# Reordered passages around a block-form dense stage: where the filler work, the PSUM banks, the weight loads and one query tile stand

## The chip, the cores and the metric

The kernel runs on one core of one Trainium2 chip. The metric is the device time of one execution in microseconds (us); lower is better. The engines are called PE (matmul), PEld (its weight loads), DVE (vector), ACT (scalar), POOL (GpSimd) and SP (the queue that issues nearly all transfers).

## The reference

Two branches of one input x (2048 rows of 640) are mixed by a gate per row, `g = sigmoid(x . gate_w)`:

```python
qkv = x @ wqkv                                # 32 heads of 20
phi(t) = [softmax(t @ w_phi), softmax(-t @ w_phi)]     # per head, for q and k
kv = phi(k).T @ v;  z = sum(phi(k))           # per head
a = (phi(q) @ kv) / (phi(q) @ z + 1e-6) @ wo
b = silu(x @ w1) @ w2                         # w1: 640 x 1728
out = g * a + (1 - g) * b
```

All of it is float32. The kernel gets near that precision by splitting an operand into a rounded high half and a low half (`split`, L117 on ACT and L119 on DVE or POOL: a cast, then a subtraction), and by three matmuls per product, high by high, high by low, low by high (`PASSES`).

## The kernel before

The work runs in four stages.

**Keys (about 0 to 173 us).** x goes by 16 tiles of 128 rows. For each tile `t` PE makes keys and values in the three PSUM banks `kvp[0..2]` (L497), DVE and ACT make the softmax features (`k_spikes`, Exp, `k_sums`), `k_split` splits them into `ph`, and two tiles later PE adds them up: `kv_acc` (L467) in five banks `kvt`, and `kv_rest` (L478) in a part of `kvp[2]`, called `krm`, which `kv_rest_sum` (L491, DVE) adds to a sum in SBUF after each tile. The table `ahead` hangs other work behind a tile: loading and splitting the first dense weights (`w_load(0)`, `w_sums(0)`, `w_parts(0, ..)`) and x for the dense stage (`n_split(b, c)`: block b of 512 rows, chunk c of 128 columns of D).

**Dense stage (about 173 to 372 us).** u = silu(x @ w1), stored to the DRAM tensor `u_d`. The 13 whole column tiles of w1 and the rest of 64 columns go two ways. The last whole tile ("l") and the rest ("r") are plain products: `h_std` (L537), 15 and 10 matmuls for a block of 512 rows. The other twelve are taken in pairs, with pairs of blocks, in a 2 x 2 block form with seven products instead of eight (a Strassen form). `h_pair(n, ..)` is one such unit, n = 0 to 11: n // 6 is the pair of blocks, n % 6 the pair of column tiles. Its seven products come in the order 1, 2, 6, 7, 4, 5, 3 (6, 9, 6, 6, 9, 9, 9 matmuls of 128 x 512: 54 in all, L583). Product 1 is copied to the tile `q` (ACT, L606); the others are added up by DVE (L597), and each of four results goes through Silu on ACT and a store (`u_out`, L548, L549). The weights of a unit are four split tiles a, b, c, d, made from two loaded tiles `wr` (L254, L255) and five POOL sums `wt` (`w_sums`, L270). The x operands are `n1`, `n2` and the split differences `t[1..4]`, made by `less` (L756) and `xt_first` for the first two blocks, and by `t_loads` (L1010), `t_sums` (POOL, L1027), `t_parts` and `n_parts` for the other two.

`between` is a table of the work that is traced behind a product of a unit (0: ahead of product 1); `plan(n)` fills it for the loads and splits of the next unit's weights. Unit 0 runs with `kvp[0]` and `kvp[1]` alone, since the key sums still hold the other banks; from unit 1 on all eight PSUM banks are used (`bank`). Ahead of unit 0 stand the two `h_std` groups of block 0 and of block 1, and the last key sums (`key_sums`) stand behind its product 1. `kv_out` (L646, L647, L652) writes the key sums out to `kv_d`. `r_out` (L553 to L556) finishes a rest group with a copy, an add, a Silu and a store.

**Queries (about 372 to 593 us).** Tiles 8 to 11 come first: `q_proj` (L455, 30 matmuls), `q_feat` (max, min, differences, Exp at L887), `q_sum`, `q_norm` (POOL, L901), `q_norm_sum` (L904), `q_small`, `q_mul` (POOL, L937), which leaves `es[t]`. Between them stand the `h_std` groups of blocks 2 and 3. `t_mm` (L1106) transposes `es` on PE, `t_out` (L1122, ACT) copies the result to `fT`, `n_mm` (L1187) multiplies with the key sums, `n_hi` and `n_lo` split that, and `w_mm` (L1220, "pa") multiplies with wo. `QT` is the list of the remaining query tiles; `step(u)` runs one group of 256 rows.

**Output (about 593 us on).** u is loaded again, split and multiplied with w2 (L1429), and the branches are mixed.

What sets the order: inside a block `with inorder(..)` the named engines run their instructions in the order of the code; each is a queue, and an instruction that waits holds up all behind it. The transfers on SP are in no such list: the planner places them by priority and by when a tile's buffer comes free, and SP then issues them one after the other, waiting where it must. A tile from a pool with `bufs` copies waits for the last reader of the copy that it takes: the pools "raw" (4), "ur" (2), "w" (9) and "u" (3) matter here.

## Time and profile before

| | us |
|---|---|
| median of 3 runs (785.01 to 786.8) | 785.77 |
| the profiled execution | 786.72 |
| its span in the profile | 784.9 |
| PE busy, share of the span | 746.2, 95% |
| PEld busy | 645.1, 82% |
| DVE busy | 448.2, 57% |
| ACT busy | 299.6, 38% |
| POOL busy | 323.4, 41% |

The mean granted clock of PE is 0.975 of full speed. Busy shares are means over stages: what a wait costs has to be read in its stage, from PE's rows in order of time. A row of PE gives its start, its length, the line, what it writes and reads, how many matmuls are merged in it, and in brackets how long PE was idle before and what released it. A merged row lasts until the end of its last matmul, which overlaps the next row a little. A row of SP lasts as long as SP was busy with or waited between the merged issues.

### The profile page before, as it was taken

The page shows a single profiled execution, that of the slowest core. Times are in us where ns is not written, and L with a number is a line of the kernel's source. Part 1 is how long each engine was busy: PE and PEld are TensorE (multiplying, and loading weights), DVE is VectorE, ACT ScalarE, POOL GpSimd, SP SyncE. Part 2 cuts the span into 40 slices and gives each one's busy share as a digit, 9 for nine tenths or more (in the row PEclk, how much of TensorE's full clock was granted, in tenths as well). Part 3 has the DMA queues.
Part 4 walks back from the last instruction along what each step waited for, and adds up shares of the span by engine and source line. Part 5 has one row for each costly group of instructions (what it writes and reads, how often), then busy time and mean ns, then how long its engine had stood idle before and what let it go on. Part 6 is the DMA issues. An engine that isn't in the chain of part 4 may idle for free.

```text
span 784.9 us, 10979 instructions
## 1 busy us (share of the span) xinstructions
PE 746.2 (95%) x4115; PEld 645.1 (82%) x4115; DVE 448.2 (57%) x760; ACT 299.6 (38%) x549; POOL 323.4 (41%) x231
## 2 busy tenths in 40 slices
PE   9999999997699979999975999999999999999997
PEld 7888888886488758888964999999998788888886
DVE  5667666786555566666865666767642452242413
ACT  5344444455334444445662353343441332111110
POOL 2479888655437633123274564563500030020300
PEclk9999999998899989999987999999999999999999
DMA  9221111101434285554310111220147676172511
GB/s 317 90 68 55 34 35 34 48 0 58 127 116 154 97 273 164 154 162 145 117 41 21 34 58 45 72 81 16 45 123 213 183 203 206 50 242 75 172 30 67
DMA packets 49663, 82.88 MB, mean 106 GB/s; under 512 B 5416, under 2 KB 18872, under 8 KB 49610
## 3 DMA queue, kind: packets, MB, share of 16 engines
q1 hardware_dynamic: 49322, 81.67, 33.5%
q8 instruction: 32, 0.52, 0.3%
q10 hardware_dynamic: 288, 0.51, 0.2%
q14 instruction: 21, 0.17, 0.1%
HBM read 56.90 MB, written 25.27 MB: 105 GB/s over the span
## 4 chain that ended last, share of the span: by engine, by line
PE 48%; DVE 4%; DMA 3%; POOL 1%; ACT 1%; issue 1%; SPq 1%; DVEq 0%; POOLq 0%; ACTq 0%
PE acc L1429 21%; PE pa L1220 9%; PE pq L455 7%; PE p L583 5%; PE pn L1187 3%; PE pT L1106 2%; DMA ur<-u_d 2%; DVE eq L446 1%; POOL eq L937 1%; DVE sm L904 1%; DMA w2rr<-w 1%; DMA u_d<-u 1%; DMA wo<-wo 1%; PE pwq L229 0%; DVE sm L891 0%
## 5 line engine op out<-in xcount | busy, mean ns | idle before, releaser
L1429 PE MATMUL acc<-u,w 128*128 128x512 f32 x780 | 178.3, 389 | 0.4 <-DVE u L119 0.2
L1429 PEld LDWEIGHTS acc<-u,w 128*128 128x128 f32 x780 | 146.3, 188 | 31.5 <-ACT u L117 0.6
L497 PE MATMUL kvp<-wh,xa 128*128 128x500 f32 (+1 forms) x420 | 92.9, 357 | 0.0
L1436 POOL TENSOR_TENSOR o<-o,y 128x512 f32<-128x512 f32 x15 | 20.1, 1374 | 149.2 <-DVE o L1435 149.2
L497 PEld LDWEIGHTS kvp<-wh,xa 128*128 128x128 f32 x420 | 71.6, 188 | 10.0
L119 DVE TENSOR_TENSOR u<-ur,u 128x512 fp32r<-128x512 f32 x52 | 36.2, 702 | 75.0 <-ACT u L117 74.8
L1220 PE MATMUL pa<-oT,wo 128*128 128x256 f32 x600 | 77.8, 283 | 0.0
L1220 PEld LDWEIGHTS pa<-oT,wo 128*128 128x128 f32 x600 | 74.2, 188 | 0.8 <-ACT oT L1196 0.8
L117 ACT CAST u<-ur 128x512 fp32r<-128x512 f32 x52 | 32.2, 623 | 107.2 <-PE acc L1429 69.1
L901 POOL TENSOR_TENSOR ez<-eq,zbc 128x1280 f32<-128x1280 f32 x16 | 46.9, 2930 | 41.5 <-ACT eq L887 29.4
L119 POOL TENSOR_TENSOR ph<-ek,ph 128x1280 fp32r<-128x1280 f32 x16 | 48.5, 3032 | 29.6 <-ACT ph L117 29.5
L548 ACT ACTIVATE u<-p 128x512 f32<-128x512 f32 x44 | 26.3, 599 | 73.6 <-issue 43.9
L937 POOL TENSOR_TENSOR eq<-eq,sm 128x1280 f32<-128x1280 f32 x16 | 37.9, 2367 | 36.0 <-DVE sm L931 35.7
L270 POOL TENSOR_TENSOR wt<-wr 128x256 f32<-128x256 f32 (+1 forms) x36 | 25.4, 705 | 66.2 <-DMA wr<-w 32.6
L497 PE MATMUL kvp<-wl,xa 128*128 128x500 f32 (+1 forms) x210 | 47.5, 356 | 0.0
L497 PEld LDWEIGHTS kvp<-wl,xa 128*128 128x128 f32 x210 | 36.3, 189 | 5.4
L525 POOL TENSOR_TENSOR ek<-ek,st 128x1280 f32<-128x1280 f32 x16 | 37.9, 2369 | 6.6 <-ACT v L316 3.6
L316 ACT CAST v<-kvp 128x360 fp32r<-128x360 f32 (+2 forms) x45 | 13.5, 337 | 69.5 <-PE kvp L497 65.9
L455 PE MATMUL pq<-wq,xn 128*128 128x320 f32 x240 | 38.7, 320 | 0.0
L455 PEld LDWEIGHTS pq<-wq,xn 128*128 128x128 f32 x240 | 37.4, 197 | 1.1 <-issue 0.8
L1122 ACT COPY fT<-pT 120x512 f32<-120x512 f32 (+1 forms) x48 | 23.5, 556 | 38.2 <-PE pT L1106 38.0
L1106 PE MATMUL pT<-ident,eq 128*120 128x128 f32 (+1 forms) x176 | 24.1, 287 | 14.0 <-POOL eq L937 8.8
(430 smaller groups left out, 1448.6 us busy)
## 6 DMA issues: line engine op xcount, KB each, us to landing
u_d<-u SPq DMA_DIRECT2D x52, 256.0 KB, 3.2
ur<-u_d SPq DMA_DIRECT2D x52, 256.0 KB, 3.7
wr<-w SPq DMA_DIRECT2D x24, 320.0 KB, 4.1
y<-fb_d SPq DMA_DIRECT2D x20, 256.0 KB, 5.1
out<-o SPq DMA_DIRECT2D x20, 256.0 KB, 4.6
w2r<-w SPq DMA_DIRECT2D x13, 320.0 KB, 4.0
fb_d<-pac SPq DMA_DIRECT2D x16, 256.0 KB, 2.1
xra<-xT SPq DMA_DIRECT2D x14, 256.0 KB, 3.0
```

The lines of the kernel that those rows point to most:

```text
L117: nc.scalar.copy(hi, src)
L119: eng.tensor_tensor(lo, src, hi.bitcast(F32), op=ALU.subtract)
L455: nc.tensor.matmul(dst, xt[c][:, hx, :], w[:, c, hw, lo : lo + n], start=first, stop=(hx == 1 and c == NC - 1))
L497: nc.tensor.matmul(kv_cols(t, lo, hi), xt[c][:, hx, :], WKV[hw][:, c, lo:hi], start=(n == 0), stop=(n == 3 * NC - 1), skip_group_check=True,)
L525: nc.gpsimd.tensor_tensor(groups(e), groups(e), spread(st[:, 1, :]), op=ALU.mult)
L548: nc.scalar.activation(o, src, AF.Silu)
L583: nc.tensor.matmul(dst, W[n][w][:, hw, j * P : (j + 1) * P], x[:, hx, :], start=(i == 0), stop=(i == len(todo) - 1))
L901: nc.gpsimd.tensor_tensor(ez, Q[t]["e"], kvb["zbc"], op=ALU.mult)
L937: nc.gpsimd.tensor_tensor(groups(q["e"]), groups(q["e"]), spread(q["sm"][:, 2 * H : 4 * H]), op=ALU.mult)
L1106: nc.tensor.transpose(pT[:w, jj * 256 + k * P : jj * 256 + (k + 1) * P], es[2 * PB[u] + k][:, j * GW : j * GW + w], ident)
L1220: nc.tensor.matmul(pa[:, a, :], WO[:, c, hw, ds] if c < NG else WOR[:, ds], o[:, ho, c, :] if c < NG else o[:GW, 0, c, :], start=(k == 0), ...
L1429: nc.tensor.matmul(acc[m], lhs, rhs, start=(f == OF[0] and n == 0), stop=(f == OF[-1] and n == len(todo) - 1))
```

## The change

It moves work; the set of matmuls stays the same.

- *Ahead of the dense stage.* The two `h_std` groups of block 1 move behind unit 0. Block 0's two groups now run unbroken, and then the sums of tile 14. Unit 0 and unit 1 each start with their products 1 and 2 in `kvp[0]` and `kvp[1]` (`h_begin`); their other five products come later (`h_rest`), when all banks are open. The last key sums stand behind product 1 of unit 1. Splits of block 1's chunks 0 and 1 move from tiles 11 and 13 to behind product 5 of unit 0; since `b12` overwrites their source, two rows of x are loaded once more (`rx1_0`, `rx1_1`). The first unit 1 weights are loaded and split at tiles 11 and 12. All `less` go to DVE, and the splits of `xt[1]` and `xt[4]` to POOL (before: `xt[3]` on POOL).
- *PSUM banks.* From `h_rest(0)` on a group takes the eight banks in a fixed turn, 0, 2, 3, 4, 5, 6, 7, 1, one buffer for each.
- *Weights.* `plan(n)` traces the load for unit n + 2 behind the last product of unit n; the buffer `wt` is taken in `w_sums`, not at the load. The x work for blocks 2 and 3 is placed behind other products.
- *Queries.* Tile 8's projection and features move into unit 11, behind product 4; the loads and splits of wo move there too, with the low halves on POOL. `pr3`, the last rest group, and the projection of the second tile of `QT` move in front of the transposes of step 1; three Silus and stores (`late_out`) come later than their sums; the fT copies stand ahead of tile 11's Exp.

The diff, cut to its core:

```diff
     def w_load(n):
...
-        s = wslot(f"wt{n}")
...
-        WR[n] = e, s
+        WR[n] = [e, None]
     def w_sums(n):
-        e, s = WR[n]
+        e = WR[n][0]
+        s = WR[n][1] = wslot(f"wt{n}")
...
+    def h_begin(n, between=None, banks=None):
...
+        p1 = banks.pop(0) if banks else bank(f"p{n}_1")
+        product(n, 1, p1)
+        if banks is None:
+            q = QS[n] = fu.tile([P, 2, 512], F32, tag="u", name=f"q{n}", bufs=3)
+            first = q[:, 0, :]
+        else:
+            first = raw(f"q{n}_0")[:, :512]
...
+        nc.scalar.copy(first, p1)
+        for part in between.get(1, ()):
+            part()
+        p2 = banks.pop(0) if banks else bank(f"p{n}_2")
+        product(n, 2, p2)
+        add(p2, p2, first)
+        u_out(2 * p, 2 * s, p2, banks is not None)
...
+    def h_rest(n, between):
...
         p6 = mm(6)
-        add(q[:, 1, :], p6, q[:, 0, :])
+        if second is None:
+            second = fu.tile([P, 2, 512], F32, tag="u", name=f"q{n}", bufs=3)[:, 1, :]
+        add(second, p6, first)
...
-        11: [lambda: n_split(1, 0, two("xn1_0"))],
-        13: [lambda: n_split(1, 1, two("xn1_1"))],
-        14: [lambda c=c: n_split(0, c, slot(f"xn0_{c}")) for c in range(4)],
+        11: [lambda: w_load(1)],
+        12: [lambda: w_parts(1, "a", "pool")],
+        13: [lambda: n_split(0, 0, slot("xn0_0"))],
+        14: [lambda c=c: n_split(0, c, slot(f"xn0_{c}")) for c in range(1, 4)],
...
+            less(b11, b12, b11)
             k_sums(t, eks[t])
...
-            h_std("l", kvp[0], n1, range(4), ends=False)
-            h_std("r", kvp[1], n1, range(4), ends=False)
+            h_std("l", kvp[0], n1, range(NC))
             for c in (2, 3):
-                n_split(1, c, home[1][:, (c + 2) * 1024 : (c + 3) * 1024].rearrange("p (s d) -> p s d", s=2))
-            h_std("l", kvp[0], n1, (4,), opens=False)
+                n_split(1, c, room(1, c + 2, 1))
             u_out(NF - 1, 0, kvp[0], True)
+            h_std("r", kvp[1], n1, range(NC))
+            phs[t] = k_split(t, eks[t])
+            r_out(0, kvp[1], True)
             kv_rest(t - 1, phs[t - 1], True)
             kv_acc(t - 1, phs[t - 1])
+            for c in range(2):
+                less(b12[:, cs[c]], b22[c], b12[:, cs[c]])
+                less(b22[c], b22[c], b11[:, cs[c]])
             kv_rest_sum(t - 1)
-            less(nc.vector, b11, b12, b11)
-            h_std("r", kvp[1], n1, (4,), opens=False)
...
-            h_std("l", kvp[0], n2, (0, 1, 4, 2, 3))
...
-            h_std("r", kvp[1], n2, range(NC))
-            r_out(1, kvp[1], True)
-            xt_first(3, "pool")
+            n_split(1, 4, slot("xn1_4"), "pool")
+            parts(xt[1], b11, "pool")
+            banks = [kvp[0], kvp[1], kvp[0], kvp[1]]
...
-            h_pair(
-                0,
-                {
-                    1: [key_sums],
-                    2: [gates, lambda: xt_first(4)],
-                    6: [lambda: w_load(1), lambda: w_sums(1)],
...
+            def two_parts():
+                for c in range(2):
+                    split(xt[2][:, 0, cs[c]], xt[2][:, 1, cs[c]], b22[c])
+
+            def four():
+                for c in range(2):
+                    less(b21[:, cs[c]], b21[:, cs[c]], b22[c])
...
+            h_begin(0, {1: [four]}, banks)
+            two_parts()
+            h_begin(1, {1: [key_sums, lambda: parts(xt[3], b12), lambda: parts(xt[4], b21, "pool")]}, banks)
+            w_sums(1)
+            kv_out()
...
+    nc.sync.dma_start(kv_d[: KF + 1], kvo[1])
+    for c in range(2):
+        rx[1, c] = raw(f"rx1_{c}")[:, :512]
+        nc.sync.dma_start(rx[1, c], x_rows(1, c)[:, 0, :])
...
     def bank(name):
-        return ps.tile([P, 512], F32, tag="bank", name=name, bufs=8)
+        k = turns["bank"] = turns.get("bank", -1) + 1
+        return ps.tile([P, 512], F32, tag=f"bank{(0, 2, 3, 4, 5, 6, 7, 1)[k % 8]}", name=name, bufs=1)
...
     def load_wo():
-            split(o[:, c, 0, :], o[:, c, 1, :], r[:, :D])
+            split(o[:, c, 0, :], o[:, c, 1, :], r[:, :D], "pool")
...
     def plan(n):
-            todo[0] += [do(w_load, n + 1), do(w_sums, n + 1)]
+            todo[0] += [do(w_sums, n + 1)]
...
+        if n + 2 < 2 * NQ:
+            todo[3] += [do(w_load, n + 2)]
...
+        h_rest(
+            0,
+            {
+                6: [do(w_parts, 1, "c")],
+                4: [do(w_parts, 1, "b")],
+                5: [do(n_split, 1, c, room(0, 4 + c, 1)) for c in range(2)],
+                3: [do(w_parts, 1, "d"), do(w_load, 2), x_open],
+            },
+        )
+        pf = bank("pf1")
+        h_std("l", pf, n1_1, range(NC))
+        u_out(NF - 1, 1, pf)
+        pf = bank("pr1")
+        h_std("r", pf, n1_1, range(NC))
+        r_out(1, pf)
         for n in range(1, NQ):
...
             if n == 1:
-                todo[0] += [x_open]
-                todo[3] += [gates_out]
+                todo[6] = todo[0]
+                todo[3] += [gates_out, do(t_loads, 0)]
-            if n in (1, 3):
-                i = n // 2
-                todo[0] += [do(t_loads, i)]
-                todo[5] += [do(n_parts, 0, i), do(n_parts, 0, 2 + i), do(t_sums, i)]
             if n in (2, 4):
                 i = n // 2 - 1
-                todo[1] += [do(t_parts, i, 1, 2)]
-                todo[5] += [do(t_parts, i, 3, 4)]
+                todo[2] += [do(n_parts, 0, i), do(n_parts, 0, 2 + i)]
+                todo[4] += [do(t_sums, i)]
+            if n in (3, 5):
+                i = n // 2 - 1
+                todo[1] += [do(t_parts, i, 1, 2, 3, 4)]
+            if n == 3:
+                todo[3] += [do(t_loads, 1)]
             if n == 5:
-                todo[0] += [do(x_raw, 2, 4), do(x_raw, 3, 4), do(x_raw, 3, 2), do(x_raw, 3, 3)]
-                todo[2] += [do(n_parts, 0, 4), do(n_parts, 1, 4)]
+                todo[2] += [do(x_raw, *bc) for bc in ((2, 4), (3, 4), (3, 2), (3, 3))]
+                todo[5] += [do(n_parts, 0, 4), do(n_parts, 1, 4)]
+            (h_rest if n == 1 else h_pair)(n, todo)
-        load_b_consts()
...
             if p == 0:
...
+                todo[5] += [load_b_consts]
...
             if p == NQ - 1:
                 todo[0] += [last_tables]
-                todo[2] += [lambda: w_odd_parts(kvb.pop("odd"))]
-                todo[4] += [make_kvw]
+                todo[1] += [lambda: w_odd_parts(kvb.pop("odd"))]
+                todo[2] += [make_kvw, load_wo]
+                todo[4] += [lambda: q_open(8, q_proj(8)), do(q_feat, 8)]
+                todo[3] += [do(xb_load, 0)]
...
         q_open(10, q_proj(10))
-        q_sum(9)
+        more(9)
         q_feat(10)
         pf = bank("pf3")
         h_std("l", pf, n2, range(NC))
-        u_out(NF - 1, 3, pf)
-        more(9)
         q_norm(10)
-        pf = bank("pr3")
-        h_std("r", pf, n2, range(NC))
+        q_open(11, q_proj(11))
         q_sum(10)
...
         for i in range(4):
             t_mm(0, i, bank)
             t_out(0, i)
+        uf3 = fu.tile([P, 512], F32, tag="ur", name="u3_12", bufs=2)
+        nc.scalar.copy(uf3, pf)
+        q_feat(11)
+        q_norm(11)
         more(10)
-        q_norm(11)
-        q_sum(11)
...
         t_all(0, range(4, 6))
+        on(0, q_mm)
         n_all(0)
-        on(0, q_mm)
-        n_out(0, range(3))
+        for gp in range(3):
+            n_hi(0, gp)
+        pf = single("pr3")
+        h_std("r", pf, n2, range(NC))
+        q_sum(11)
+        more(11)
+        on(1, q_mm)
+        late_out(NF, 2, ur2, FR)
+        late_out(NF - 1, 3, uf3)
+        ur3 = r_sum(3, pf)
+        late_out(NF, 3, ur3, FR)
+        for gp in range(3):
+            n_lo(0, gp)
...
         on(0, q_logits)
-        more(11)
         on(0, q_norm, q_sum)
```

126 lines of the change are left out of this document (51 added, 75 removed).

## The prediction

> **What bounds the kernel now.** I read the page's shares and slices first, then who TensorE (PE) waited for, then PE in order of time around the thin slices, then the other engines there.
>
> ```profile
> PE 746.2 (95%) x4115; PEld 645.1 (82%) x4115; DVE 448.2 (57%) x760; ACT 299.6 (38%) x549; POOL 323.4 (41%) x231
> PE   9999999997699979999975999999999999999997
> PEclk9999999998899989999987999999999999999999
> ```
>
> PE is the bound. Its thin slices (about 19.6 us each) are numbers 10, 11, 15, 21 and 22, the passages that the change touches, and the granted clock drops in the same places. Who PE waits for, in total (us, times, longest), three of its rows:
>
> ```profile
> PE pT L1106 <- POOL eq L937: 8.8, 2, 8.6
> PE kvp L583 <- DVE q L597: 3.7, 1, 3.7
> PE p L583 <- ACT u L548: 3.4, 2, 3.1
> ```
>
> In order of time (start, us, what, idle before it and its releaser); the ws3a and ws4a rows are the undisturbed measure:
>
> ```profile
> 187.15 1.33 PE L467 MATMUL kv<-ph,v 128*121 128x256 f32 x10
> 192.70 4.21 PE L583 MATMUL kvp<-xn,ws0a 128*128 128x512 f32 x9 [4.22 <-DVE u_r L554]
> 215.47 5.30 PE L583 MATMUL p<-xn,ws1a 128*128 128x512 f32 x15 [3.07 <-ACT u L548]
> 229.48 3.69 PE L583 MATMUL p<-xn,ws2a 128*128 128x512 f32 x15
> 241.84 3.56 PE L583 MATMUL p<-xn,ws3a 128*128 128x512 f32 x15
> 254.09 3.56 PE L583 MATMUL p<-xn,ws4a 128*128 128x512 f32 x15
> 268.06 3.72 PE L583 MATMUL p<-xn,ws5a 128*128 128x512 f32 x15 [1.58 <-ACT ws5a L117]
> 283.98 1.85 PE L583 MATMUL p<-xn,ws6a 128*128 128x512 f32 x4 [3.36 <-ACT ws6a L117]
> 300.95 3.67 PE L583 MATMUL p<-xn,ws7a 128*128 128x512 f32 x15
> 397.00 4.56 PE L455 MATMUL pq<-wq,xn 128*128 128x320 f32 x30
> 408.92 1.54 PE L1106 MATMUL pT<-ident,eq 128*120 128x128 f32 x6 [5.25 <-ACT fT L1122]
> 428.37 2.39 PE L1106 MATMUL pT<-ident,eq 128*120 128x128 f32 x10 [8.60 <-POOL eq L937]
> 430.40 6.47 PE L455 MATMUL pq<-wq,xn 128*128 128x320 f32 x30
> 436.71 1.25 PE L1106 MATMUL pT<-ident,eq 128*120 128x128 f32 x10
> 437.72 2.02 PE L1220 MATMUL pa<-oT,wo 128*128 128x256 f32 x15
> 441.69 2.81 PE L1187 MATMUL pn<-fT,kvw 120*64 120x256 f32 x24
> ```
>
> A pair's 54 matmuls take 254.09 - 241.84 = 12.25 us, 0.227 each. By that measure three passages lose:
> - A, from the key sums' end (188.48) to pair 2 (229.48): 41.0 us for 48 + 54 matmuls, worth 23.1: 17.9 lost.
> - B, pairs 2 to 6: 300.95 - 229.48 = 71.5 for 61.25: 10.2 lost.
> - C, 397.00 to 437.72: 40.7 us. Its work is three query tiles (4.4 each), 44 transposes (0.10 each, from 436.71 to 437.72) and 24 pn (2.74): 20.3. Lost 20.4.
>
> Together 48.5 us; no gain in these passages can exceed it. Part is no idle time: after the 3.07 gap 15 matmuls took 5.14 against 3.40, after the 1.58 gap 3.56, and after the 8.60 gap 30 took 6.31 against 4.40. So I price a gap above 3 us at its length plus 1.7 to 2 of half clock, a gap below 2 at its length.
> [...]
>
> **The change part by part.** I lay the rows' durations in the new order, engine by engine, in the clock of the trace before. The rows that decide A and B (the two stretches give the busy time of PE, PEld, DVE, ACT and POOL, then granted clock, DMA share and GB/s):
>
> ```profile
> 154.87 2.37 POOL L525 TENSOR_TENSOR ek<-ek,st 128x1280 f32<-128x1280 f32 x1 [0.39 <-DVE st L524]
> 155.31 2.48 DVE L119 TENSOR_TENSOR xn<-rx,xn 128x512 fp32r<-128x512 f32 x1
> 174.58 2.54 POOL L119 TENSOR_TENSOR xn<-rx,xn 128x512 fp32r<-128x512 f32 x2
> 180.83 1.21 DVE L756 TENSOR_TENSOR rx<-rx,rx 128x1024 f32<-128x1024 f32 x1
> 180.84 4.02 POOL L119 TENSOR_TENSOR ph<-ek,ph 128x1280 fp32r<-128x1280 f32 x1 [1.38 <-ACT ph L117]
> 194.32 2.37 POOL L119 TENSOR_TENSOR xs<-rx,xs 128x1024 fp32r<-128x1024 f32 x1 [6.97 <-ACT xs L117]
> 200.00:210.00 10.00, 6.26 (x21) 4.65 (x21) 6.05 (x11) 2.31 (x4) 7.07 (x10) 0.83 0.44 124
> 230.00:240.00 10.00, 10.00 (x45) 8.26 (x44) 5.36 (x8) 5.08 (x11) 7.79 (x7) 1.00 0.31 114
> 266.28 0.62 ACT L117 CAST xt<-xr 128x512 fp32r<-128x512 f32 x1 [1.66 <-POOL xr L1027]
> 282.82 2.15 DVE L119 TENSOR_TENSOR xn<-xr,xn 128x512 fp32r<-128x512 f32 x2 [2.36 <-DMA xr<-xT]
> 309.04 0.58 ACT L606 COPY q<-p 128x512 f32<-128x512 f32 x1
> 322.41 0.58 ACT L606 COPY q<-p 128x512 f32<-128x512 f32 x1
> ```
>
> **Free edits.** w_load(1) and the split of ws1a move to tiles 11 and 12: two DMA issues on SP, past the rx and xra loads, one ACT cast and one POOL subtract of about 1.6 us, in POOL's spare time of that tile; without that cover ph is 1 us later, and its reader is two tiles off. One n_split fewer at tile 14 gives DVE 0.6. The two reloads of rx1 (256 KB each) meet DMA engines 0.44 busy at 200 to 210, but SP issues them in order: behind a store that still waits they slip, priced in A. The wo low halves go from DVE to POOL (5 x 1.6), which is free from 370.7 to 382.8.
>
> **A.** Each step is a wait of PE in the new order.
> 1. The l group of h_std runs unbroken, so chunk 4 of block 0 is wanted at 175.7; its low half comes from POOL, behind ph, with the first less (1.21) now beside it: about 176.9. Gap 0.9.
> 2. r, then the sums of tile 14, end at 181.0, the first product of pair 0 at 182.3. The second needs kvp[1] back from r_out, whose ACT copy stands behind the ph cast: 182.8. Gap 0.5.
> 3. DVE then has four less of 512 (0.6 each) and, only behind them, kv_rest_sum(14), for which the tile 15 sums wait. DVE and POOL block each other where both read SBUF: the 0.69 us subtract at 155.31 took 2.48 beside POOL's, and POOL's ph took 4.02, not 2.96, beside DVE's less. Taking turns with ph (2.96), xn1_4 (1.28) and xt1 (2.37), the fourth less ends at 190.5, the sum at 190.9. PE was done with pair 1's first product at 187.05: gap 3.9. If DVE gets its four in a row it is 187.4 and the gap 0.4.
> 4. Pair 1's second product waits for kvp[1]: four (1.2), add (0.7), Silu (0.6): 193.4. Gap 1.0.
> 5. p6 of pair 0 takes bank 0, but p7 takes bank 2, that of kvp[2], whose last reader is kv_rest_sum(15) in kv_out. On the way lie xt2, the q copy, xt3, an add, a Silu, five kv copies and adds: 200.9. PE is idle from 196.8: gap 4.1.
> 6. 33 matmuls of pair 0, slow at first, end near 210.4; block 1's chunk 0, split behind p5's add and Silu, is there at 210.7. Then 25 + 39 matmuls (14.5): pair 2 at 226, against 229.48.
>
> [...]
>
> So A gives 3.5. DVE first in step 3 makes it 7; rx1 loads stuck behind the kv_d store, which waits for POOL's mask products, make pair 2 2.5 later, and another half-clock stretch 3: -2. I take 4, nearer the order as written.
>
> **B.** ACT and DVE run behind PE here: pair 7's first product ends at 302.3, its q copy comes at 309.04. A pair's weights can be some 4 us late before PE waits for them (PE has six us of work after the product behind which they are split, the split takes 2), and the stalls at ws5a and ws6a come where an ACT cast of xt has stood 1.66 for POOL's t_sums and a DVE split 2.36 for a DMA. The new plan loads raw x a pair earlier, puts t_sums two products ahead of its readers, and loads x four products ahead of its split. From one q copy to the next ACT and DVE take 13.4 us (322.41 - 309.04), of which 2.4 are an n_parts pair of splits and the wq parts; so 11 bare, 12.3 with n_parts, 13.3 with four t_parts, 14.6 with both. Pairs 2 to 6 come to 64.8, against PE's 61.25: a lag of 3.5 at the end, about what the slack covers. I expect 2 lost: a gain of 8. The w_load of pair n+2 stands where the load for it stood before, at the end of pair n, and takes the slot that the same product frees, so the weights may come no sooner: then only the two waits go, a gain of 4. Upper end: all 10.
>
> **C.** These rows carry it (the first: the u stores, with the us from issue to landing):
>
> ```profile
> u_d<-u SPq DMA_DIRECT2D x52, 256.0 KB, 3.2
> 368.33 1.57 POOL L119 TENSOR_TENSOR w_l<-w1l,w_l 128x640 fp32r<-128x640 f32 x1 [9.00 <-ACT w_l L117]
> 382.80 2.96 POOL L901 TENSOR_TENSOR ez<-eq,zbc 128x1280 f32<-128x1280 f32 x1 [12.06 <-issue]
> 406.99 1.27 ACT L887 ACTIVATE eq<-eq 128x1280 f32<-128x1280 f32 x1
> 408.28 2.05 ACT L1122 COPY fT<-pT 120x512 f32<-120x512 f32 x4
> 425.95 2.36 POOL L937 TENSOR_TENSOR eq<-eq,sm 128x1280 f32<-128x1280 f32 x1
> ```
>
> Before, the fT copies stand behind tile 11's Exp, and es of tile 11 comes at 428.3, behind QT0's logits on DVE. After: tile 8 in the last pair starts the feature chain 4 us earlier, the fT copies stand ahead of that Exp, more(11) ahead of QT0's logits, and pr3 (2.3 us) and a second query tile (4.4) lie in front of the transposes. The chain then runs: es of 9 at 398.6, Exp 11 at 406.1, es of 10 at 413.4, es of 11 at 417.7; PE reaches that transpose at 418.6, or 420.5 if slow. That wait goes. Two others stay:
> - Transpose 5 needs a bank whose fT copy ends at 404.1, and QT0 one of tile 11: PE waits 3.7 from 400.5.
> - Next late: ACT now has three Silus, two table loads, a copy of ur3 that waits for the store of ur2 (two "ur" buffers, 3.2 us to landing) and QT0's Exp ahead of the next fT copies. Those come near 427, and the fifth transpose of step 1 takes their bank. PE waits 6 there, then about 2 of half clock.
>
> The pa products start near 430, not 437.7: 7.5 gained. Without the store's wait it is 10.5, with all of it hidden 15, and 4 if the feature chain is 3 us longer.
>
> **Sum.** 4 + 8 + 7.5 = 19.5 off the span of 784.9: 765.4. The profiled execution's 786.72 is 1.8 above its span and 0.95 above the 785.77 median. So 766.3 by median: 766.
>
> **The rivals.**
> - *More is regained* (0.2). DVE wins step 3 and kv_out comes before p7: A gives 12, B 10, C 11: 753. For it: PE has work at every wait. Against: steps 4 and 5 are data and bank waits in series.
> - *A gives nothing back* (0.17). Steps 3 and 5 each cost 3 more and a slow stretch, 10 worse than forecast, and B gives only its 4: 780. For it: two banks, kvp[0] and kvp[1], carry four products and two h_std groups in turn.
> - *Banks in turn stall the dense stage* (0.09), the other side. Before, a group takes any free bank of eight; now only its own, behind the group eight earlier. Where ACT and DVE lag more than seven groups PE idles; at 3 us (1.7 more slow) a stall costs 4.8, so from five stalls in eleven pairs it is slower, at seven 800. Against: PE waited for a Silu in the dense stage only 3.4 in total with lags of 7, and groups are freed in nearly that order.
> - *The weights come no sooner* (0.1): B gives 4, total 770, inside the forecast's range.
>
> [...]
>
> **How the numbers follow.** The forecast has 0.44, with its own range 757 to 774 from the ends of A, B and C. The range 750 to 780 takes in the first, second and fourth rival and leaves the third out and the far ends: about 2 in 10. A difference under 0.2% (1.6 us) is what this kernel's measurement can't tell from none. Faster: all but the third rival and the tail of the second, 0.88. Same 0.03, slower 0.09.
>
> **What would show it.** After: no ws5a or ws6a wait; PE's wait on eq L937's counterpart gone; one wait of 3 to 5 at the second product after the keys' end or at p7 of pair 0 (releaser DVE, the kra sum); pair 2 near 226; a wait on an fT copy in step 1. Wrong if pair 2 starts after 230, if PE waits on a Silu in pairs 3 to 10, or if the clock is under 0.95 there.

## The result, and the profile after

The changed kernel takes 779.83 us (median of 8 runs, 777.22 to 783.47), the kernel before 785.42 in the same series (8 runs, 783.89 to 788.15): ratio 0.9927, 95% interval 0.9901 to 0.9952. It is 5.6 us faster, where 19.5 were forecast. The profiled execution took 781.32, its span is 779.5, 5.4 under the 784.9 of before.

The page of the changed kernel, PE's shares and the slices:

```profile
PE 744.7 (96%) x4115; PEld 643.4 (83%) x4115; DVE 451.9 (58%) x755; ACT 296.2 (38%) x548; POOL 331.8 (43%) x236
PE   9999999997899869999997999999998999999997
PEclk9999999999899979999998999999999999999999
```

Slices are 19.5 us. Number 10 is as thin as before, 11 and 22 are thicker, 21 is full. But 14 and 15 (253 to 292 us, units 4 to 6 of the dense stage) are thin, 15 also slow (0.7), and 31, where the output stage begins, is a little thin. Who PE waits for, the changed kernel (us, times, longest):

```profile
PE p L583 <- ACT xn L117: 7.2, 1, 7.2
PE pT L1139 <- ACT fT L1155: 5.6, 2, 4.5
PE kvp L478 <- DVE kra L491: 3.4, 1, 3.4
PE acc L1477 <- DVE pac L1271: 2.8, 1, 2.8
PE p L583 <- DVE ws5a L119: 2.1, 1, 2.1
```

The 8.8 us on POOL's `eq` is gone. At the top stands a wait that the kernel before did not have, and the fourth is new too. PE in order of time, the changed kernel, at the marks of the three passages and at the output stage:

```profile
190.64 0.34 PE L478 MATMUL kvp<-ph,v 128*121 128x228 f32 x1 [3.42 <-DVE kra L491]
192.99 4.21 PE L583 MATMUL kvp<-xn,ws1a 128*128 128x512 f32 x9 [0.83 <-ACT u L548]
201.09 1.63 PE L583 MATMUL p<-xs,ws0c 128*128 128x512 f32 x6 [1.59 <-DVE kra L491]
225.15 3.69 PE L583 MATMUL p<-xn,ws2a 128*128 128x512 f32 x15
263.28 1.19 PE L583 MATMUL p<-xn,ws5a 128*128 128x512 f32 x4 [1.13 <-ACT ws5a L117]
266.59 4.38 PE L583 MATMUL p<-xn,ws5a 128*128 128x512 f32 x11 [2.11 <-DVE ws5a L119]
289.48 3.35 PE L583 MATMUL p<-xn,ws6a 128*128 128x512 f32 x7 [7.22 <-ACT xn L117]
302.41 3.56 PE L583 MATMUL p<-xn,ws7a 128*128 128x512 f32 x15
425.72 1.54 PE L1139 MATMUL pT<-ident,eq 128*120 128x128 f32 x6 [4.47 <-ACT fT L1155]
426.91 3.55 PE L1256 MATMUL pa<-oT,wo 128*128 128x256 f32 x15
432.79 2.81 PE L1223 MATMUL pn<-fT,kvw 120*64 120x256 f32 x24
587.15 18.91 PE L1477 MATMUL acc<-u,w 128*128 128x512 f32 x75 [2.85 <-DVE pac L1271]
```

Laid against the rows of before, one execution each, the marks say where the 5.4 us come from (start of each, us; the last three columns are experiments, below):

| mark | before | changed | held | held, seam | before, held |
|---|---|---|---|---|---|
| unit 2 | 229.48 | 225.15 | 226.28 | 224.97 | 230.19 |
| unit 7 | 300.95 | 302.41 | 289.04 | 287.74 | 299.35 |
| unit 11 | 357.82 | 358.60 | 345.22 | 343.93 | 355.57 |
| the pn behind the first pa | 441.69 | 432.79 | 418.66 | 417.02 | 437.44 |
| first output group | 593.06 | 587.15 | 573.10 | 568.39 | 588.79 |
| end of the span | 784.9 | 779.5 | 765.5 | 759.1 | 779.6 |

A gained 4.3. Units 2 to 6 (B) took 77.3 instead of 71.5: all of A was lost again, and 1.5 more. Units 7 to 10 gave 0.7. From unit 11 to pn (C) 9.7 were gained. The queries behind it lost 3.0, by the new wait for `pac`, and the output stage 0.5. Sum: 4.3 - 5.8 + 0.7 + 9.7 - 3.0 - 0.5 = 5.4. Against the forecast (4, 8 and 7.5, and nothing elsewhere) 14.1 us are missing: 13.8 in B and 3.5 behind C, less small gains in the other parts.

### The profile page after: what moved, and what is told of

It reads as the page before. It is cut to its first block, busy times and chain, and to the rows that moved or that the text cites. A ratio compares the mean times of both kernels' runs of the same rounds, so it can differ in the third digit from the quotient of the medians.

```text
span 779.5 us, 10978 instructions
## 1 busy us (share of the span) xinstructions
PE 744.7 (96%) x4115; PEld 643.4 (83%) x4115; DVE 451.9 (58%) x755; ACT 296.2 (38%) x548; POOL 331.8 (43%) x236
## 4 chain that ended last, share of the span: by engine, by line
PE 56%; DMA 3%; DVE 3%; ACT 2%; issue 2%; POOL 1%; SPq 0%; DVEq 0%; ACTq 0%; POOLq 0%
PE acc L1477 24%; PE p L583 10%; PE pa L1256 9%; PE pq L455 7%; PE pn L1223 3%; PE pT L1139 2%; DMA xr<-xT 1%; PE pwq L229 1%; DMA w2rr<-w 1%; DMA wr<-w 1%; DVE eq L446 0%; DMA u_d<-u 0%; ACT eq L899 0%; PE pf L537 0%; POOL wt L270 0%
## 5 line engine op out<-in xcount | busy, mean ns | idle before, releaser
L1256 PE MATMUL pa<-oT,wo 128*128 128x256 f32 x600 | 79.6, 287 | 0.0
L119 DVE TENSOR_TENSOR u<-ur,u 128x512 fp32r<-128x512 f32 x52 | 36.1, 701 | 73.5 <-ACT u L117 73.4
L1256 PEld LDWEIGHTS pa<-oT,wo 128*128 128x128 f32 x600 | 76.1, 193 | 0.8 <-ACT oT L1232 0.8
L117 ACT CAST u<-ur 128x512 fp32r<-128x512 f32 x52 | 32.2, 623 | 107.9 <-PE acc L1477 75.1
L1483 DVE TENSOR_TENSOR o<-acc,G 128x512 f32<-128x512 f32 x20 | 13.7, 692 | 41.4 <-PE acc L1477 33.4
L455 PE MATMUL pq<-wq,xb 128*128 128x320 f32 x240 | 37.2, 312 | 0.0
L455 PE MATMUL pq<-wq,xn 128*128 128x320 f32 x240 | 36.8, 310 | 0.1
L455 PEld LDWEIGHTS pq<-wq,xn 128*128 128x128 f32 x240 | 35.6, 188 | 1.1 <-issue 0.4
```

The lines of the kernel that those rows point to most:

```text
L117: nc.scalar.copy(hi, src)
L119: eng.tensor_tensor(lo, src, hi.bitcast(F32), op=ALU.subtract)
L455: nc.tensor.matmul(dst, xt[c][:, hx, :], w[:, c, hw, lo : lo + n], start=first, stop=(hx == 1 and c == NC - 1))
L1256: nc.tensor.matmul(pa[:, a, :], kvb["wo"][:, c, hw, ds] if c < NG else WOR[:, ds], o[:, ho, c, :] if c < NG else o[:GW, 0, c, :], start=(k ...
```

## The experiments

All are timed against the kernel before on the same chip, in five rounds. "Units 2 to 6" is the time from the start of unit 2 to that of unit 7 in the profiled execution (71.5 before, 77.3 changed). One execution is a rough measure of it: four of the runs below leave the work of these units as the changed kernel has it, and took 75.6 (seam), 75.6 (cback), 78.7 (tfront) and 81.1 (kra). A difference of two or three us decides nothing by itself.

**First reading.** In the changed kernel the rows of B show DVE subtracts stretched while POOL works through x (1.77 us for ws3c, where ws2c, of the same shape, took 0.68 at 222.13 with POOL idle), and chunk 4 of x late. POOL and DVE of the changed kernel, by time:

```profile
233.06 6.57 POOL L1040 TENSOR_TENSOR xr<-xr,xr 128x512 f32<-128x512 f32 x4 [0.63 <-DVE xn L119]
```
```profile
234.90 1.89 DVE L119 TENSOR_TENSOR ws3a<-wr,ws3a 128x640 fp32r<-128x640 f32 x1
236.71 1.77 DVE L119 TENSOR_TENSOR ws3c<-wt,ws3c 128x512 fp32r<-128x512 f32 x1
```

So the first four runs took the sums away, moved chunk 4, gave the banks back their free choice, and moved the output stage's first bank.

*nosum* (leaves out the POOL subtractions of `t_sums`, four in each of its two calls, so that the differences of x are not formed):
```diff
-        for o, x, y in ((b11, b12, b11), (b12, b22, b12), (b22, b22, b11), (b21, b21, b22)):
-            nc.gpsimd.tensor_tensor(o, x, y, op=ALU.subtract)
```


> The changed kernel without the eight POOL subtractions of t_sums: the differences of x for blocks 2 and 3 are left out, their splits read the raw rows. Theory (DVE and POOL block each other): the DVE splits of ws3a, ws3c, ws5a and ws5c, which take 0.9 to 1.9 us beside t_sums, fall to 0.7 to 0.8, ACT's and DVE's lag at unit 5 shrinks by 3 to 4 us, PE's waits at ws5a (1.1 and 2.1) go, and the 7.2 wait shrinks to 3 to 5: 5 to 8 us less than the changed kernel. Rival (the lag has other causes): the splits are short, but PE's waits stay within 1 us.

Measured: 775.06, ratio 0.9863 (0.9837 to 0.9889); units 2 to 6 72.3. The waits for ws5a shrank from 3.2 to 1.3, the 7.2 stayed at 7.3. The time is near the theory's, but it had the 7.2 shrink to 3 to 5.

*x4* (chunk 4 loaded and split in unit 3, not unit 5):
```diff
+                todo[1] += [do(x_raw, 2, 4), do(x_raw, 3, 4)]      # n == 3
+                todo[5] += [do(n_parts, 0, 4), do(n_parts, 1, 4)]  # n == 3
```


> The changed kernel, but chunk 4 of blocks 2 and 3 is loaded behind product 1 of unit 3 and split behind its product 5, two units earlier; nothing else in the plan moves. Theory (order): PE's wait of 7.2 on the xn cast in unit 6 goes with its slow stretch of about 3, unit 7 starts near 293 and not 302.4: 7 to 10 us less than the changed kernel, 770 to 773; some 3 us at ws5a stay or grow by 1, since unit 3 is loaded more. Rival (the banks in turn or the later weight loads hold pairs 5 and 6): another wait of the same size takes its place, unit 7 stays after 300.

Measured: 778.01, 0.9895 (0.9874 to 0.9916); units 2 to 6 73.5. The 7.2 fell to 1.0, but the wait for ws5a grew from 1.1 to 4.5. Unit 7 starts at 298.2, between the two theories. Part of the work taken from one place was waited for at another.

*freebank* (a group takes any free bank):
```diff
-        return ps.tile([P, 512], F32, tag=f"bank{(0, 2, 3, 4, 5, 6, 7, 1)[k % 8]}", name=name, bufs=1)
+        return ps.tile([P, 512], F32, tag="bank", name=name, bufs=8)
```


> The changed kernel with the banks of the dense stage taken as before the change: one pool of eight, any free one, no fixed turn. Theory (order of the x work): units 2 to 6 as in the changed kernel, unit 7 within 1 us of 302.4 counted from unit 2; the start of unit 0's rest may move by 2 us either way, as its first two groups get other banks. Rival (the fixed turn costs units 2 to 6 their gain): unit 2 to unit 7 falls from 77.3 us to below 72.

Measured: 778.69, 0.9909 (0.9881 to 0.9937); units 2 to 6 78.7. The fixed turn of banks is not the cause.

*seam* (the output stage's eight banks begin at 1):
```diff
+    for k in range(8):
+        ps.tile([P, 512], F32, tag=f"acc{k}", name=f"orderacc{k}", bufs=1)
-            acc = [ps.tile(.., tag="acc", .., bufs=8) for m in range(NC)]
+            acc = [ps.tile(.., tag=f"acc{(b * NC + m + 1) % 8}", .., bufs=1) for m in range(NC)]
```


> The changed kernel, but the accumulators of the output stage take the eight PSUM banks in a fixed turn that starts at bank 1, not at the bank which the last wo group (pa) held. Theory (the added rest group pr3 takes one more turn of the four single banks, so the last pa group now sits in the bank that the first output accumulator takes, and PE waits for its copy): PE's wait of 2.8 on the pac copy goes, and with it the slow clock behind it (75 matmuls took 18.9 us, before the change 17.2): 4 to 4.7 us less than the changed kernel, about 775.5. Rival (DVE is late in any case and the first matmuls wait for the u splits): the wait moves to another releaser, under 1 us gained.

Measured: 776.12, 0.9877 (0.9855 to 0.9898). PE's first output row in it, to set beside the 18.91 and 2.85 above:

```profile
581.65 17.18 PE L1479 MATMUL acc<-u,w 128*128 128x512 f32 x75
```

The wait is gone, and with it 1.7 us of slow clock (in the changed kernel the granted clock was 0.66 from 587.15 to 592.15; before, without the wait, 1.00 over the first 5 us). The added `single("pr3")` shifted the turn of the four query banks by one, so the last pa group stood in the bank that the first output group takes.

**Second round: is it the x plan?**

*oldx* (the x plan of units 1 to 6 as before the change; its core):
```diff
+                todo[6 if n == 1 else 0] += [do(t_loads, i)]                                   # n in (1, 3)
+                todo[5] += [do(n_parts, 0, i), do(n_parts, 0, 2 + i), do(t_sums, i)]           # n in (1, 3)
+                todo[0] += [do(x_raw, 2, 4), do(x_raw, 3, 4), do(x_raw, 3, 2), do(x_raw, 3, 3)]  # n == 5
+                todo[2] += [do(n_parts, 0, 4), do(n_parts, 1, 4)]                              # n == 5
```


> The changed kernel, with the loads, sums and splits of the second half's x in units 1 to 6 at the places that they had before the change; all else is as changed. The theory (the new x plan costs what the dense stage lost): the stretch from unit 2 to unit 7 falls from 77.3 to about 71.5 us, the 7.2 us wait for the xn cast in unit 6 goes, and the time is near 774. The rival (the stretch lost its time to the weights loaded a pair ahead, or to banks in turn): it stays at 76 to 78 us and the time within 1 us of the 779.8 of the changed kernel.

Measured: 779.93, 0.9916 (0.9883 to 0.9948); units 2 to 6 75.2. The stretch is between the two theories, the time is the rival's: the 7.2 went, but waits for ws4a (2.5), ws5a (1.9) and ws6a (4.0) took its place.

*x4u1* (chunk 4 in unit 1):
```diff
-                todo[6] = todo[0]
+                todo[6] = todo[0] + [do(x_raw, 2, 4), do(x_raw, 3, 4)]      # n == 1
+                todo[5] += [do(n_parts, 0, 4), do(n_parts, 1, 4)]           # n == 1
```


> The changed kernel, with chunk 4 of blocks 2 and 3 loaded behind product 6 of unit 1 and split behind its product 5, and not in unit 5. The theory (the 7.2 us wait hangs on raw buffers that POOL frees late, and DVE and ACT lag only from unit 2 on): the wait for the xn cast falls under 1.5 us, the waits for ws5a stay near 3.2, units 2 to 7 take about 69 us and the time is 772. The rival (DVE and ACT are full over the whole stretch, as it looked when the same splits stood in unit 3): the waits for ws5a grow to 4.5 or more, units 2 to 7 take 73.5 and the time is 777.

Measured: 779.86, 0.9922 (0.9895 to 0.9948); units 2 to 6 73.3. PE in it:

```profile
266.25 2.08 PE L583 MATMUL p<-xn,ws5a 128*128 128x512 f32 x4 [3.50 <-ACT ws5a L117]
294.81 2.77 PE L583 MATMUL p<-xn,ws6d 128*128 128x512 f32 x9 [0.85 <-ACT xn L117]
```

The rival held in the stage: the 7.2 is 0.9 now, and ws5a waits 3.5 and 1.3. The time is 3 us above the rival's 777: of the 3.8 us that unit 11 came sooner the fT copies of the queries took most back.

*x4u1_dve* (also the sums of raw x on DVE):
```diff
-            nc.gpsimd.tensor_tensor(o, x, y, op=ALU.subtract)
+            nc.vector.tensor_tensor(o, x, y, op=ALU.subtract)
```


> As x4u1, with the eight subtractions of the sums of raw x on DVE, not on POOL. With the four of a set left out units 2 to 7 were 5.0 us shorter. If what they cost is the turn-taking of DVE and POOL (two splits of 0.7 and 0.8 us that became 1.8 and 1.9 in each set), four subtractions of 0.7 us on DVE cost as much as they save: within 1 us of x4u1, 772. If POOL's own lateness is what is waited for (6.1 to 6.6 us for a set there, 2.8 on DVE), the waits for ws5a fall under 1.5 us and the time is 769. If DVE is full, they grow by 1.2 us and the time is 774.

Measured: 779.69, 0.9908 (0.9886 to 0.993); units 2 to 6 75.0. POOL had 13.9 us less to do between 190 and 326 us than in x4u1, and the time is the same. This is what was expected of the turn-taking: a set of four subtractions costs DVE 2.86, and its splits of ws3a and ws3c are 2.2 shorter together (0.81 and 0.69, not 1.91 and 1.78). So the run moves no work off DVE on balance, and can't tell the turn-taking from a chain in which DVE's work is a link.

*kra* (`kv_rest_sum(14)` ahead of the four less; a line moved up past them):
```diff
+            kv_rest_sum(t - 1)
...
-            kv_rest_sum(t - 1)
```


> The changed kernel, with the rest sum of tile 14 ahead of DVE's four less of the last key tile. The theory (step 3 of A, DVE and POOL in turns, makes the 3.4 us wait of PE at 190.6): that wait falls under 0.6 us. What is late next is the same chain on DVE, so I expect about 1.5 us of it back at the next products and unit 2 some 1 to 2 us sooner, the time 778. The first rival (the wait is PE's own way to the bank): 3.4 stays. The second rival (nothing else is in series): unit 2 comes 3.4 plus 1.5 of slow clock sooner, near 220.5, and the time is 775.

Measured: 780.23, 0.9931 (0.9905 to 0.9957). PE in it:

```profile
192.84 4.21 PE L583 MATMUL kvp<-xn,ws1a 128*128 128x512 f32 x9 [4.22 <-ACT u L548]
200.94 2.81 PE L583 MATMUL p<-xs,ws0c 128*128 128x512 f32 x6 [2.18 <-DVE kra L491]
```

The 3.4 went and the next wait grew from 0.8 to 4.2: the first theory's mechanism held, but nothing was left over: unit 2 starts at 226.63, not 1 to 2 sooner. (Where A is as in the changed kernel, the runs have this mark between 224.6 and 226.4.)

**What these have in common.** Put PE's waits aside and follow ACT. Its copy `q` of product 1 comes once in a unit. From that of unit 2 to that of unit 7 pass 75.3 us before, 76.2 changed, 75.7 in oldx, 75.9 in x4u1, 77.5 in x4u1_dve, 76.7 in x4, 74.8 in seam, and 74.3 to 79.2 in freebank, kra and three runs of the next rounds (cback, wearly, tfront); 71.9 in nosum alone, where work was left out. The first and last of the changed kernel:

```profile
229.65 0.57 ACT L606 COPY q<-p 128x512 f32<-128x512 f32 x1
305.84 0.58 ACT L606 COPY q<-p 128x512 f32<-128x512 f32 x1
```

Wherever the x work stands, five units of ACT and DVE take 74 to 79 us, PE's matmuls 61.3. Yet neither engine is full: DVE is busy for 52.5 of the 77.3 us, ACT for 34.0 (changed kernel, the stretch of units 2 to 6; the columns are PE, PEld, DVE, ACT, POOL, granted clock, DMA share, GB/s):

```profile
225.15:302.41 77.26, 66.48 (x272) 53.34 (x271) 52.48 (x71) 33.97 (x67) 42.34 (x41) 0.91 0.54 171
```

What fills the rest shows in the rows, DVE's and then ACT's, of the changed kernel:

```profile
253.69 1.10 DVE L119 TENSOR_TENSOR ws4b<-wr,ws4b 128x384 fp32r<-128x384 f32 x1 [1.11 <-ACT ws4b L117]
255.65 0.68 DVE L588 TENSOR_TENSOR p<-p,r 128x512 f32<-128x512 f32 x1
257.45 0.56 DVE L119 TENSOR_TENSOR ws4d<-wt,ws4d 128x384 fp32r<-128x384 f32 x1 [1.11 <-ACT ws4d L117]
257.92 0.69 DVE L588 TENSOR_TENSOR p<-p,r 128x512 f32<-128x512 f32 x1
```
```profile
256.42 0.60 ACT L548 ACTIVATE u<-p 128x512 f32<-128x512 f32 x1 [2.46 <-issue]
256.91 0.50 ACT L117 CAST ws4d<-wt 128x384 fp32r<-128x384 f32 x1
258.70 0.60 ACT L548 ACTIVATE u<-p 128x512 f32<-128x512 f32 x1 [1.28 <-issue]
```

The profile names no releaser for these two Silus ("issue"); for the one in the same place a unit earlier it does:

```profile
244.67 0.60 ACT L548 ACTIVATE u<-p 128x512 f32<-128x512 f32 x1 [1.28 <-DVE p L588]
```

DVE adds p; ACT's Silu follows; behind the Silu stands the cast of a weight part; DVE, in order, waits 1.11 for that cast (the Silu and the cast fill this time, 256.42 to 257.41), subtracts, and only then adds the next p, for which ACT waits 1.28. In units 2 to 6 DVE waits so for a cast sixteen times (1.1 to 1.7 us). The product was ready long before (the Silu at 256.42 is of unit 3, whose matmuls ended at 249.7). Two engines hand one thread to each other.

**The test of it.** *hold*: each DVE subtract of a weight or x part is issued one product later, behind the next product's adds. Nothing else in the code moves.
```diff
+        if lo_eng == "held":
+            held.append(lambda: nc.vector.tensor_tensor(lo, src, hi.bitcast(F32), op=ALU.subtract))
+            return
...
         def after(k):
+            flush()          # issues what is held; also behind product 2
             for part in between.get(k, ()):
```


> The changed kernel, with the DVE subtract of each weight part and of each raw x part of units 1 to 11 issued one product later than its ACT cast, behind the next product's adds; the work and its place on ACT, POOL and the queues are as changed. The earlier runs that moved x work left the time from ACT's q copy of unit 2 to that of unit 7 at 74.8 to 77.5 us (before 75.3, changed 76.2), against 61.3 of matmuls. The theory (a serial chain, in which DVE waits 1.1 us for each cast and the adds and Silus of the next product stand behind the subtract, bounds units 2 to 6): without these waits that stretch falls under 68 us, no wait of PE for ws5a or ws6a is left, unit 2 to unit 7 falls from 77.3 to between 62 and 70 (the 7.2 us wait for the last x cast may stay), and the time is 766 to 773. [...] A second rival (the weights' load, issued 3 to 5 us into the unit ahead, sets the pace): the waits for ws5a stay, but with no lag of DVE; above 775.

Measured: 767.13 (766.51 to 767.87), 0.9755 (0.9737 to 0.9772). Units 2 to 6 took 62.8 us. The same stretch, its first and last q copies and the subtracts of unit 4's weights in it:

```profile
226.28:289.04 62.76, 61.81 (x273) 50.63 (x271) 48.29 (x65) 32.10 (x64) 42.97 (x41) 1.00 0.61 187
```
```profile
227.96 0.59 ACT L615 COPY q<-p 128x512 f32<-128x512 f32 x1
295.93 0.58 ACT L615 COPY q<-p 128x512 f32<-128x512 f32 x1
```
```profile
247.62 1.80 DVE L125 TENSOR_TENSOR ws4a<-wr,ws4a 128x640 fp32r<-128x640 f32 x1
249.34 1.77 DVE L125 TENSOR_TENSOR ws4c<-wt,ws4c 128x512 fp32r<-128x512 f32 x1
252.23 0.54 DVE L125 TENSOR_TENSOR ws4b<-wr,ws4b 128x384 fp32r<-128x384 f32 x1
253.64 0.54 DVE L125 TENSOR_TENSOR ws4d<-wt,ws4d 128x384 fp32r<-128x384 f32 x1
```

No bracket stands behind them. Of DVE's sixteen waits for casts three are left in the stretch, two for parts of x (1.18 and 0.64) and one, near its end, for ws7c (1.98); most of its other waits are for PE's products. Of PE's waits one, of 0.95, is left, and the clock is 1.00. The subtracts beside POOL still take 1.8, so their length there was not what bound; it only lengthened the links of a chain. Expected was a stretch of q copies under 68; it is 67.97, just inside: ACT and DVE still fall behind PE's 61.3, but PE no longer has to wait for it.

In the changed kernel ws4c took 1.77 beside POOL (250.19 us), against the 0.68 of ws2c. The adds of L588, with one input in PSUM and one in SBUF, took 0.68 to 0.69 beside POOL's `t_sums` (233.50, 234.29 and 238.40 us), so the forecast's "where both read SBUF" is wider than these rows. Beside POOL the subtracts of hold are as long as those of the changed kernel, and the stage is 14.5 us shorter.

*wearly* (the load of unit n + 2 behind product 7):
```diff
-            todo[3] += [do(w_load, n + 2)]
+            todo[7] += [do(w_load, n + 2)]
```


> The changed kernel, with the load of the weights of unit n+2 behind product 7 of unit n, not behind its last product. The theory of a serial chain on ACT and DVE: the load is not what units 2 to 6 wait for; the stretch from unit 2 to unit 7 stays at 75 to 78 us and the time within 1.5 us of 779.8. The rival (the load, which lands 10 to 11 us into the unit ahead and is followed by 3.5 us of sums, sets the pace): the waits for ws5a go, the stretch falls by 5 us and the time to 775.

Measured: 780.01, 0.9919 (0.9902 to 0.9935); units 2 to 6 78.5, the waits for ws5a 1.1 and 2.2. Loading sooner gains nothing: the load is not the pace.

*before_hold* (the same edit in the kernel before; the held x subtracts are issued ahead of `t_sums`, which overwrites what they read):
```diff
-                todo[5] += [do(n_parts, 0, i), do(n_parts, 0, 2 + i), do(t_sums, i)]
+                todo[5] += [do(n_parts, 0, i), do(n_parts, 0, 2 + i), flush, do(t_sums, i)]
```


> The kernel before, with the held subtracts alone (each DVE subtract of a weight part or raw x part of units 1 to 11 one product behind its ACT cast). The theory (the serial chain of ACT and DVE made the 10.2 us that the kernel before lost in units 2 to 6): unit 2 to unit 7 falls from 71.5 to about 63 us, the waits for ws5a and ws6a go, and the time is near 777; hold, at 767.1, stays 9 to 11 us faster, which is what the change gives elsewhere. The rival of the prediction (those waits came from the x loads and POOL's sums standing late in ACT's and DVE's order): unit 2 to unit 7 stays above 69 us and the time above 783.

Measured: 781.02, 0.993 (0.9908 to 0.9952); units 2 to 6 69.2, which is the rival's side of its bound, with a time between the two theories. Up to unit 6 it was as the first said (279.28 against 283.98). Then ACT waited, and PE for it:

```profile
293.68 0.60 ACT L557 ACTIVATE u<-p 128x512 f32<-128x512 f32 x1 [7.95 <-DMA u_d<-u]
294.18 1.13 ACT L123 CAST xn<-xr 128x512 fp32r<-128x512 f32 x2
```

So the chain alone does not account for what the kernel before lost in units 2 to 6: holding the subtracts saves 2.3 us of that stage there, where it saves 14.5 in the changed kernel.

*hold_oldx* (the diffs of hold and oldx, with that `flush`):


> The held subtracts in the changed kernel, with the loads, sums and splits of the second half's x in units 1 to 6 at the places that they had before the change. With its new plan it took 62.8 us from unit 2 to unit 7 and 767.1 in all; the kernel before with the held subtracts 69.2, with 7.95 us of a Silu waiting for its buffer's store while four x loads stood in the queue. The theory (the new x plan is worth those 6.4 us once the chain is no bound): 68 to 70 us from unit 2 to unit 7, the time 773 to 774. The rival (they come from the weights' load a pair ahead or from banks in turn): within 1.5 us of 62.8 and of 767.1.

Measured: 771.43 (771.19 to 772.11), 0.9809 (0.9782 to 0.9836); units 2 to 6 69.1, with the same Silu waiting 7.48 for its store. The stretch is as the theory said; the time is 2 us better than expected. So the new x plan is worth 6.4 us there, 4.3 in all, once the chain is no bound. Which part of the plan it is was not tested; the loss that shows is the Silu's wait for its store. While the chain bound, oldx and the changed kernel took the same 779.9 and 779.8.

**Passage C.**

*cback* (`more(11)` back behind the logits of QT0):
```diff
-        more(11)
         on(1, q_mm)
...
         on(0, q_logits)
+        more(11)
```


> The changed kernel, with the weighting of query tile 11 back behind the logits of QT0. The theory (what passage C gained is the wait for es of tile 11, which was on the path before): es of 11 comes at about 428.5, not 417.4, PE waits 8 to 9 us before the 16 transposes at 418.9, pa starts 6 or 7 us later, near 433, and the time is 786. The rival (C gained by its filling, pr3 and a query tile ahead of the transposes, and not by the earlier es): pa starts less than 2 us later and the time is 781.

Measured: 784.62, 0.9987 (0.9965 to 1.001), on the same chip as hold. Its wait:

```profile
427.82 4.42 PE L1139 MATMUL pT<-ident,eq 128*120 128x128 f32 x20 [10.25 <-POOL eq L949]
```

From unit 11 to pa 75.1 us against 68.3. The earlier es of tile 11 is worth 4.8 of C's gain by the medians (of two series).

*tfront* (the first fT copies of step 1 ahead of QT0's logits; `step(1)` then leaves them out):
```diff
+        t_all(1, range(3))
         on(0, q_logits)
```


> The changed kernel, with the first three transpose groups of step 1 and their fT copies written ahead of the logits of QT0, so that on ACT these copies stand ahead of that tile's Exp. The theory (the 4.5 us wait of PE ahead of the fifth transpose is ACT's order): it falls under 1.5 us, with it 1.9 us of slow clock; pa starts near 421.5 and the time falls by 5 to 774 or 775. The rival (the copies wait for their own transposes and banks): the wait stays above 3 us and the time above 778. What would be late next is es of QT0, some 2 us later than 433.5, which is wanted only in step 2.

Measured: 779.9, 0.9917 (0.9897 to 0.9938). The 4.5 went, pa came 5.0 sooner after unit 11, and two later waits took most of it back:

```profile
433.94 6.21 PE L455 MATMUL pq<-wq,xn 128*128 128x320 f32 x30 [2.59 <-DVE sm L943]
447.61 1.31 PE L1139 MATMUL pT<-ident,eq 128*120 128x128 f32 x10 [1.54 <-POOL eq L949]
```

What I named as late next was right in kind (QT0's features), but what waits first is a query projection in step 1, not step 2.

**Together.** *hold_seam* has the diffs of hold and seam, *hold_seam_tf* that of tfront too:


> The held subtracts, with the output stage's banks begun at 1, as in seam. The theory (the two losses are apart, in series on PE): the 2.9 us wait for pac at the first output group goes with 1.7 of slow clock, as it did alone (3.7 by the medians), and the time is 763 to 764. The rival (what is won at one place is waited for at the next): within 1 us of 767.1.

> As hold_seam, with the first fT copies of step 1 ahead of QT0's logits, as in tfront. Alone that took 5.0 us from the start of pa and gave 2.6 and 1.5 us back at the next two waits, so that unit 11 to the output stage was 2.1 us shorter. The theory (that remainder is real): 2 us less than hold_seam, 761 to 762. The rival (all of it is given back): the same as hold_seam.

Measured: hold_seam 762.33 (760.87 to 763.16), 0.9692 (0.9667 to 0.9717), the fastest version here, 4.8 under hold, measured in another series (3 to 4 were expected). hold_seam_tf 762.6, 0.9698: all that tfront wins is given back (from unit 11 to the first output group 224.5 us in the one, 224.4 in the other).

## Why the prediction was right or wrong

**Direction and range** held (faster; 779.83 in 750 to 780, by 0.2 us); the size did not: 5.6 of 19.5. That it stayed in the range is luck, since the passage that was to give most lost time. Two of the signs named for a wrong forecast came in B: waits for ws5a, and a clock of 0.91 in units 2 to 6, under the 0.95.

**A was right.** Unit 2 starts at 225.15, forecast 226 (step 6 as written, 210.7 and 14.5, adds up to 225.2). Step 3 was put at 3.9 and measured 3.42. Step 5 was put at 4.1 and measured 1.6, but before it 9 matmuls took 4.21 us at a granted clock of 0.50, 2.2 more than 9 at 0.227 each. The four less of the turn-taking are one row of 7.50. kra shows that step 3 is a place, not a price: the chain through DVE and ACT ends as late without it.

**B failed, in sign.** The step was "ACT and DVE take 11 bare, 12.3 with n_parts, 13.3 with four t_parts, 14.6 with both; pairs 2 to 6 come to 64.8". Measured are 76.2. The rows that I quoted held the warning: 13.4 us from one q copy to the next where no sums of x stood, against PE's 12.25. I took 2.4 of busy time off that and called the rest bare. But in a chain that passes between two engines, a link costs its wait too: 1.1 for each weight cast. With these waits gone hold takes 67.97, 3.2 above the forecast's sum and not 11.4. So the lag did not grow by 3.5 in five units; from a unit's start to its q copy it grew from 4.5 us in unit 2 to 12.25 in unit 5 (263.28 to 275.53), by 7.8 in three, beyond the slack of 4. Two things follow. A's 4.3 could not be kept, because unit 7 waits for a chain, not for PE. And chunk 4, loaded two products later and split four products later in that chain, became a wait of 7.2, of which x4 and x4u1 recover only part before the chain takes its place. This is also where the changed kernel falls behind the kernel before, which has the same chain: from q copy to q copy it is only 0.9 us longer (76.2 against 75.3), but before, PE started unit 7 8.1 us ahead of its q copy (300.95 and 309.04), and here 3.4 (302.41 and 305.84).

That the new x plan is worth something in B is right: hold_oldx prices it at 6.4, against the 8. It was hidden behind a second bound of nearly the same length. The mechanism that I gave (raw x earlier, sums ahead of their readers) is not shown by that; the row that shows a loss there is a Silu waiting for its store, which I had not named. The rival "the weights come no sooner" was right on the load, which issues 2.7 to 6.7 us into units 3 to 6 (before 3.1 to 6.7), and wearly shows that loading sooner gains nothing. "Banks in turn stall the dense stage" fell with freebank, and with hold, where the turn is kept and PE waits 0.95.

**C was right in mechanism, undersized.** The rows of the changed kernel, POOL's and then ACT's:

```profile
415.04 2.37 POOL L949 TENSOR_TENSOR eq<-eq,sm 128x1280 f32<-128x1280 f32 x1
```
```profile
416.82 0.58 ACT L1165 COPY u_r<-pr 64x512 f32<-64x512 f32 x1 [1.96 <-DMA u_d<-u_r]
423.79 1.27 ACT L899 ACTIVATE eq<-eq 128x1280 f32<-128x1280 f32 x1 [2.98 <-DVE eq L446]
425.08 2.78 ACT L1155 COPY fT<-pT 120x512 f32<-120x512 f32 x6
```

es of 11 was put at 417.7 and comes at 417.4; the fT copies were put near 427 and start at 425.1. The terms too large were the store's wait (3.2, measured 1.96), the wait at the transposes of 400 (3.7, measured 1.1) and the one ahead of the fifth transpose (6, measured 4.5). By the mark of the forecast, the first pa, C gained 11.6 from unit 11, against 7.5; at pn 9.7 is left, since the clock is still slow there (0.50 granted from 426.91 to 430.40; the first 15 pa matmuls took 3.55 us, before 2.02 at 1.00).

**The output seam was not in the sum at all.** Adding a tile to a fixed turn of banks shifts every later tile; I followed the turn only through the dense stage. Its wait cost 3.0, and the slow clock behind it up to 1.7 more (75 matmuls in 18.91 us, before 17.21); by the medians seam is 3.7 faster. In the other runs that keep this turn the wait is 1.3 to 3.1 us, and the slow clock came only in those of 2.43 and more (75 matmuls in 18.88 us behind 2.87 in hold and 18.86 behind 3.08 in x4u1, but in 17.30 behind 2.40 in cback).

With hold the three steps can be added again: 784.9 less 765.5 is 19.4, but it is another sum than mine, with a better B and the seam's loss in it.

## What to carry to other kernels

Where PE waits in a stage, measure the period of the chain behind it (one instruction that comes once a unit, from first to last) and set it beside PE's own; if the period is the same however the work is ordered (74 to 79 us for five units here, against PE's 61.3), the chain binds, and moving work only moves the wait. Take it from several executions: here it spread by 5 us. In such a chain a cast on one engine and its subtract on another should not stand back to back in order: put the subtract one product later, so that neither engine waits for the other (in hold sixteen such waits of DVE became three). When a buffer is added to a fixed turn, follow the turn to the next stage.

## What was not expected of the hardware

- No engine was full, and yet a chain bound: DVE 68% and ACT 44% busy in units 2 to 6, PE idle or slow for 16 of 77 us. Without the 1.1 us waits the same work fits in 62.8 us at a granted clock of 1.00, not 0.91.
- The time spread more in the changed kernel (777.2 to 783.5 in 8 runs) than in hold (766.5 to 767.9 in 5). That the chain is the reason is not shown: wearly, which has it too, lies between 779.2 and 780.9 in 5.
- In these runs the slow clock does not follow from the length of a gap. Behind the same wait of 3.42 or 3.43 (the `kra` row) the nine matmuls of ws1a took from 2.55 (wearly) to 4.21 us (changed, with 0.83 more of waiting between), and behind the same 4.22 those of ws0a took 4.21 in the kernel before and 3.36 in before_hold. Behind one wait of 1.92 (oldx, unit 5) the granted clock fell to 0.70 and 0.65 over the next 5 us; behind waits of 0.88 and 2.19 in the same place (cback) it stayed at 1.00. So the forecast's price by length, a gap below 2 at its length alone, does not hold here.
